# Decode attention with its gradients: Wq's rows kept beside the zeros of the fills, all moments in one tile, V of one group read again

## The chip, the cores and the metric

The kernel runs on one core of a Trainium2 chip. The metric is the device time of one execution in microseconds. Below, PE is TensorE (the matmuls), DVE VectorE, ACT ScalarE, POOL GpSimd and SP SyncE. DMA transfers are issued from the queues of SP, ACT and POOL, and 16 DMA engines carry them all. SBUF has 128 partitions.

## The reference

A transformer block for one token (D = 448) and its gradients. The forward pass, cut to what matters:

```python
W = min(4096, max(256, Sk // 4))               # window of 4096 out of Sk = 32768
q = x_norm @ wq                                # 16 heads of 256, 8 groups of K and V
k, v = k_cache[:, :, Sk - W:], v_cache[:, :, Sk - W:]
p = softmax(q k^T / 16);  o = p v
h  = x + o @ wo
h2 = h + ((norm(h) @ w_gate) * (norm(h) @ w_up)) @ w_down
```

The outputs are h2 and the gradients of x, of both caches and of the five weights. The gradients of the caches (out_2 for K, out_3 for V) have the caches' full size, 8 groups of 32768 x 256 in bf16, 134 MB each. They differ from zero only in the last 4096 positions of each group; the other 28672 have to be written as zeros. That is 235 MB of the 281 MB that the kernel writes.

## The kernel before

**Fills.** The tile `zeros` is [128, 8192] in bf16, 16 KB a partition (line 75). DVE sets its partitions 32 to 95 to zero (L77). A fill (L81) is one DMA that writes a stretch of zeros: its source are the 16 partitions 32, 36, ..., 92 (`ALL`, line 85), each repeated, and one DMA packet is one row of 16 KB. Fifteen of the sixteen regions (a group of out_2 or out_3, 14.7 MB each) are one DMA each on SP's queue. The sixteenth is dealt out in unequal parts per DMA engine, some on SP and some on POOL (`deal`, `deal_all`, `deal_rest`, lines 93 to 117); `deal_rest(0)` is issued after out_0 and `deal_rest(1)` after the last other store.

**SBUF.** One large tile, BIG, is cut into slots of 16 KB a partition. Slots 0 to 7 hold V of groups 0 to 7, slots 8 and 9 alternate for K (`KS = 8`); slot 4 on holds Wq at the start, when V of the later groups isn't there yet. Behind the slots lie a ring of small buffers and 896 columns of Wq that stay (`wq_kept`, KW).

**Stage 1** (0 to about 250 us). Wq is loaded in two DMAs on SP ahead of the fills and one on ACT (lines 67 to 69). In the layout of Wq each partition has 28 KB, seven rows of 2048 columns (NI = 7, HQ = 2048). Layernorm, then q in 112 matmuls (L306). For every group g: scores (K transposed by PE, L341, then L346), softmax, and `moments(g)`, which sums V^T (p K) over the window in 32 steps into a 256 x 512 product (L398), together with o and the mean of K (L401, L404). The loads of K and V go through POOL's queue, in program order, each when its slot is free. The products of the groups 4 to 7 are kept in `Mt` [128, 4, 2, 512]; those of groups 0 to 3 are spread in quarters over the partitions 0 to 31 and 96 to 127 of `zeros`, which no fill reads (`quarter`, L414 and L415).

**Stage 2** (to about 420 us). Wo, the two gate weights and w_down are loaded into the slots of K (`load_wo`, `load_wd`); out_0; then the gradients back to dh, dO and dq. `to_rows` and the broadcasts (L557, L570, L627) bring columns into rows. The quarters are copied back into `Mq` (L585). dq uses the moments (L612).

**Stage 3** (to about 667 us). For each group, 32 matmuls make the rows of dK and dV (`d_ps`, L764) into a pair of slots (`PAIR`), which two DMAs on POOL store. Beside them, `during` deals the outer products that are the gradients of the weights over the steps of the loop, one instruction after each matmul, and their stores go to POOL's queue. The gradient of x needs Wq once more: two loads on POOL in steps 2 and 3 (`dxn_load`), eight products on DVE (L658) in steps 3 and 4.

**Order.** The order on each engine is that of the program, except where `issue_after` names a predecessor. `io_load` chains the loads of POOL.

Of the kernel before, what the change touches and what calls it, by code (L numbers as in the profile page):

```python
# [14 lines left out]
D = 448  # L15
NI = 7
# [14 lines left out]
NZ = (Sk - W) * Dh // (128 * ZW)  # L31


KS = 8
TAIL = 10 * SLOT
KW = 896
RING = TAIL + 6016
SIZE = RING + KW
# [4 lines left out]
def kernel(  # L43
# [21 lines left out]
    wq_sb = BIG[:, 4 * SLOT:4 * SLOT + NI * HQ]  # L65
    wq_kept = BIG[:, RING:SIZE]
    for c0, c1 in ((KW, 4 * HQ), (4 * HQ, NI * HQ)):
        FILL.dma_start(out=wq_sb[:, c0:c1], in_=flat_rows(A_wq)[:, c0:c1])
    S_.dma_start(out=wq_kept, in_=flat_rows(A_wq)[:, 0:KW])

    def wq_at(i, c0, n):
        c = i * HQ + c0
        return wq_kept[:, c:c + n] if c < KW else wq_sb[:, c:c + n]

    zeros = const.tile([128, ZW], bf16)
    for p in (32, 64):
        V_.memset(zeros[p:p + 32, :], 0.0)  # L77
# [7 lines left out]
    ALL = slice(32, 93, 4)  # L85
    for g in range(G):
        for o in (out_2, out_3):
            if (g, o) != (G - 1, out_3):
                fill(FILL, region(o, g), ALL, 8 * NZ, ZW)
# [30 lines left out]
    GQ = G // 2  # L120
    Mt = const.tile([128, GQ, 2, 2 * Dh], bf16)
    ME = 4 * Dh

    def quarter(a):
        p = 96 * (a // 2)
        return zeros[p:p + 32, :].rearrange("p (g b c) -> p g b c", b=2, c=ME)[:, :, a % 2, :]
# [11 lines left out]
    Vw = [slot_kv(g) for g in range(G)]  # L138
# [27 lines left out]

    load_K(0)
# [11 lines left out]
    ones_f = const.tile([128, 128], f32)  # L179
    V_.memset(ones_f[:], 1.0)  # L180
# [23 lines left out]
    Par = const.tile([2, 2, 128], bf16)  # L204
    nc.gpsimd.memset(Par[:], 0.0)
    for i2 in range(2):
        pv = Par[:, i2, :].rearrange("s (m e) -> s m e", e=2)
        nc.gpsimd.affine_select(out=pv, in_=pv, compare_op=ALU.not_equal, fill=1.0, base=-i2,
                                pattern=[[0, 64], [1, 2]], channel_multiplier=2 * i2 - 1)
# [14 lines left out]
    def rows_to_half(row):  # L224
        t = ps.tile([128, NI], f32, tag="tmp", bufs=1)
        xe = small.tile([1, 2, 128], f32, tag="R", name="xe")
        for i in range(NI):
            c = xe[:, i % 2, :]
            V_.tensor_copy(out=c.rearrange("o (m r) -> o m r", r=2), in_=half_cols(row, i))
            P_.matmul(t[:, i:i + 1], lhsT=c, rhs=ones_f[0:1, 0:1], start=True, stop=True)  # L230
        return t
# [12 lines left out]
    def total(parts, n):  # L244
        t = ps.tile([128, n], f32, tag="tmp", bufs=1)
        P_.matmul(t[:], lhsT=ones_f[:], rhs=parts, start=True, stop=True)
        return t
# [24 lines left out]
    def layernorm_bwd(Pp, xh, rstd, extra, gain, tag):  # L272

        st = small.tile([128, 2], f32, tag="lb_st", bufs=1)
        V_.reduce_sum(out=st[:, 0:1], in_=Pp, axis=AX)
        jk = small.tile([128, NI], f32, tag="lb_j", bufs=1)
# [3 lines left out]
        t = small.tile([128, NI], f32, tag="lb_t", bufs=1)  # L280
# [21 lines left out]

    q_ps = ps.tile([128, 2, 16], f32, tag="tmp", bufs=1)
    for b in range(16):
        for i in range(NI):
            P_.matmul(q_ps[:, :, b], lhsT=wq_at(i, b * 128, 128), rhs=xx1[:, i, :], start=(i == 0), stop=(i == NI - 1))  # L306
# [52 lines left out]
    def softmax(g):  # L359
# [10 lines left out]
        P_.matmul(nb[:], lhsT=ones_f[0:2, :], rhs=gd[:], start=True, stop=True)  # L370
# [13 lines left out]
    def moments(g):  # L384
# [26 lines left out]
        if g < GQ:  # L411
            for a in range(4):
                q = quarter(a)[:, g, :].rearrange("p (f c) -> p f c", f=2)
                S_.copy(out=q[:, 0, :], in_=MT[0][32 * a:32 * a + 32, :])  # L414
                V_.tensor_copy(out=q[:, 1, :], in_=MT[1][32 * a:32 * a + 32, :])  # L415
        else:
            S_.copy(out=Mt[:, g - GQ, 0, :], in_=MT[0][:])
            V_.tensor_copy(out=Mt[:, g - GQ, 1, :], in_=MT[1][:])
# [34 lines left out]
    for g in range(G):  # L453
# [3 lines left out]
        if g + 3 < G:  # L457
            load_V(g + 3)
        if g == G - 2:
            load_wo(0, 18)  # L460
        if g == 0:
# [4 lines left out]
            P_.matmul(t[:], lhsT=ones_f[0:1, :], rhs=go_f, start=True, stop=True)  # L466
            S_.copy(out=dh2_bc[:], in_=t[:])
    load_wo(18, 32)
# [85 lines left out]
    def to_rows(blocks, src, nb, b0, n):  # L554
        t = ps.tile([2, 4, 128], f32, tag="tmp", bufs=1, name="t")
        for j in range(n):
            P_.matmul(t[:, j, :], lhsT=src[:, b0 + j:b0 + j + nb + 1:nb], rhs=ident_bf[:], start=True, stop=True)  # L557
        evac(blocks, t[:, 0:n, :])

    P2 = const.tile([128, 2, NI], f32)  # L560
    for w, w_sb in ((0, wg_sb), (1, wu_sb)):
        r = small.tile([2, HF], bf16, tag="R", name="r")
        r_m = r[:].rearrange("s (j m) -> s m j", m=NI)
        for b0 in (0, 4):
            n = min(4, NI - b0)
            to_rows(r_m[:, b0:b0 + n, :], dgu[:, w, :], NI, b0, n)
        for i2 in range(2):
            for x in range(0, HF, D):
                bc = ps.tile([128, D], f32, tag="tmp", bufs=1, name="bc")
                P_.matmul(bc[:], lhsT=Par[:, i2, :], rhs=r[:, x:x + D], start=True, stop=True)  # L570
                evac(bc2[w][:, i2, x:x + D], bc[:])
# [11 lines left out]
    Mq = wu_sb[:, 0:GQ * ME].rearrange("p (g c) -> p g c", c=ME)  # L583
    for a in range(4):
        S_.copy(out=Mq[32 * a:32 * a + 32], in_=quarter(a))  # L585
# [4 lines left out]
    doT_f = const.tile([128, 32], f32)  # L590
# [9 lines left out]
    q_rows = zeros[0:H, 0:Dh]  # L600
    do_rows = zeros[0:H, Dh:2 * Dh]
    rows16(qT, q_rows, SCALE)
    rows16(doT, do_rows, 1.0)

    dq_ps = ps.tile([128, 32], f32, tag="tmp", bufs=1, name="dq_ps")
    for h in range(H):
        for dk in range(2):
            for hf in range(2):
                c0 = (h % 2) * Dh + dk * 128
                g = h // 2  # L610
                m = Mq[:, g, hf * 2 * Dh + c0:hf * 2 * Dh + c0 + 128] if g < GQ else Mt[:, g - GQ, hf, c0:c0 + 128]
                P_.matmul(dq_ps[:, 2 * h + dk:2 * h + dk + 1], lhsT=m, rhs=doT[:, 2 * h + hf:2 * h + hf + 1],  # L612
                          start=(hf == 0), stop=(hf == 1))
# [6 lines left out]
    late = Mt[:].rearrange("p g f c -> p (g f c)")  # L620
    dq_bc = late[:, 0:2 * HQ].rearrange("p (i c) -> p i c", i=2)
    for b1 in range(0, 16, 4):
        r = small.tile([2, 4, 128], bf16, tag="R", name="r")
        to_rows(r[:], dq[:], 16, b1, 4)
        for i2 in range(2):
            bc = ps.tile([128, 512], f32, tag="tmp", bufs=1, name="bc")
            P_.matmul(bc[:], lhsT=Par[:, i2, :], rhs=r[:].rearrange("s b c -> s (b c)"), start=True, stop=True)  # L627
            evac(dq_bc[:, i2, b1 * 128:b1 * 128 + 512], bc[:])
    tps_cm.__exit__(None, None, None)
# [17 lines left out]
    Pq = const.tile([128, NI + 1], f32)  # L647
    wq2 = [slot(3 + i // 4)[:, (i % 4) * HQ:(i % 4 + 1) * HQ] for i in range(NI)]

    def wq_from(i):  # L650
        return 0 if i else KW

    def dxn_load(i0, i1):
        c = wq_from(i0)
        IO.dma_start(out=slot(3 + i0 // 4)[:, c:(i1 - i0) * HQ], in_=flat_rows(A_wq)[:, i0 * HQ + c:i1 * HQ])

    def wq_product(w, i, c, n):
# [164 lines left out]
```

## Time and profile before

| | |
|---|---|
| median of 3 runs | 778.72 us (778.43 to 779.66) |
| the profiled execution | 779.32 us, its span 777.5 us |
| busy: PE, DVE, ACT, POOL | 468.0, 402.0, 177.1, 43.3 us |
| TensorE's granted clock, mean | 0.657 |
| DMA | 330.44 MB, mean 425 GB/s |
| queue of SP | 230.94 MB |
| queue of POOL | 98.59 MB |
| HBM read, written | 49.15 MB, 280.59 MB |

In the profile a group of instructions is named by its line (L764), engine, operation and tile. The table of 40 slices gives the busy share of each engine in tenths, the clock that TensorE was granted, and the busy share and rate of the DMA engines. The queues' rows give packets, MB and the time that the packets took as a share of the 16 engines' span. A row of a DMA issue ends with the microseconds from issue to landing.

### The profile page before, as it was taken

To read this page: it belongs to the slowest core of one execution; us is meant where nothing else is said; L and a number is where in the kernel's file an instruction comes from. 1 tells how busy PE (TensorE), PEld (TensorE's weight loads), DVE (VectorE), ACT (ScalarE), POOL (GpSimd) and SP (SyncE) were. 2 spreads that over 40 slices of the span, in tenths; PEclk is the share of its full clock that TensorE was granted. 3 is DMA by queue.
4 is the path that set the end of the run, shared out by engine and by line. 5 is a ranking of instruction groups with operands and counts; after the bars stand their busy time and mean duration, and the time that the engine had idled before them with its cause. 6 is when DMAs were issued, how large, how long until landed. Compare 5 with 4: busy or idle time off the path is not lost.

```text
span 777.5 us, 10855 instructions
## 1 busy us (share of the span) xinstructions
PE 468.0 (60%) x4375; PEld 257.5 (33%) x4420; DVE 402.0 (52%) x1179; ACT 177.1 (23%) x278; POOL 43.3 (6%) x88
## 2 busy tenths in 40 slices
PE   4798898899899612234076998980957598200000
PEld 3654554565555311113052443430333232000000
DVE  5477677677667311255954656667577377200000
ACT  0322322321120000034333444440413244100000
POOL 3000000000000000010000001000001010100000
PEclk9998998999999855555555555555555555555555
DMA  9999999999999999999999999999999999999998
GB/s 363 427 425 428 426 425 430 428 426 428 424 428 429 429 430 430 433 430 430 424 428 430 430 429 430 428 427 431 428 430 429 429 427 431 430 433 432 428 429 349
DMA packets 25683, 330.44 MB, mean 425 GB/s; under 512 B 3069, under 2 KB 3199, under 8 KB 5046
## 3 DMA queue, kind: packets, MB, share of 16 engines
q1 hardware_dynamic: 14557, 230.94, 69.6%
q0 software_dynamic: 10928, 98.59, 30.1%
q8 instruction: 34, 0.56, 0.3%
q10 hardware_dynamic: 148, 0.23, 0.1%
q14 instruction: 16, 0.12, 0.0%
HBM read 49.15 MB, written 280.59 MB: 424 GB/s over the span
## 4 chain that ended last, share of the span: by engine, by line
PE 40%; DMA 28%; DVE 13%; issue 4%; ACT 2%; another core or an unknown queue 2%; POOL 0%; POOLq 0%; DVEq 0%; ACTq 0%
PE MT L398 12%; DMA out_dram<-BIG 10%; PE tr L341 8%; PE d_ps L764 7%; DMA BIG<-in_B_w_down_dram 7%; DMA BIG<-in_A_wq_dram 6%; DMA BIG<-in_A_k_cache_dram 4%; DVE BIG L588 2%; PE sT L346 2%; DMA BIG<-in_A_wo_dram 2%; DVE BIG L574 1%; PE dp L346 1%; DVE zeros L415 1%; ACT BIG L291 1%
## 5 line engine op out<-in xcount | busy, mean ns | idle before, releaser
L764 PE MATMUL d_ps<-BIG 32*128 32x512 bf16 x256 | 121.8, 607 | 41.3 <-ACT BIG L291 23.9
L398 PE MATMUL MT<-BIG 128*128 128x512 bf16 x467 | 140.4, 409 | 2.1 <-DVE BIG L394 0.4
L394 DVE TENSOR_SCALAR BIG<-BIG,pf 128x256 bf16<-128x256 bf16 x512 | 114.3, 282 | 29.0 <-PE MT L398 26.0
L291 ACT CAST BIG<-d_ps 128x512 bf16<-128x512 f32 x156 | 88.9, 587 | 154.9 <-PE d_ps L764 121.6
L341 PE MATMUL tr<-ident_bf,BIG 128*128 128x128 bf16 x1024 | 113.1, 268 | 14.7 <-DVE doW L588 12.6
L341 PEld LDWEIGHTS <-BIG 128*128 128x128 bf16 x1024 | 80.8, 120 | 43.4 <-issue 41.4
L293 DVE COPY BIG<-tr 128x1024 bf16<-128x1024 bf16 x92 | 63.3, 688 | 43.6 <-PE tr L341 43.3
L293 DVE CAST BIG<-d_ps 128x512 bf16<-128x512 f32 x100 | 68.0, 684 | 16.5 <-DMA out_dram<-BIG 8.2
L291 ACT COPY BIG<-tr 128x1024 bf16<-128x1024 bf16 x36 | 36.4, 1012 | 127.8 <-PE tr L341 120.5
L346 PEld LDWEIGHTS <-BIG 128*128 128x128 bf16 x1024 | 37.4, 102 | 80.1 <-DVE BIG L293 53.3
L401 PEld LDWEIGHTS <-BIG 128*128 128x128 bf16 x512 | 42.2, 99 | 52.9 <-issue 16.9
L401 PE MATMUL acc<-pT_all,BIG 128*128 128x2 bf16 x512 | 45.0, 164 | 16.6 <-DVE kbar L420 15.0
L398 PEld LDWEIGHTS <-BIG 128*128 128x128 bf16 x512 | 40.5, 103 | 23.8 <-issue 16.8
L404 PE MATMUL acc<-pT_all,BIG 128*128 128x2 bf16 x512 | 44.3, 164 | 0.0
L764 PEld LDWEIGHTS <-BIG 32*128 32x128 bf16 x256 | 21.3, 113 | 65.9 <-issue 46.4
L346 PE MATMUL dp<-doT,BIG 128*128 128x2 bf16 x512 | 24.4, 168 | 12.2 <-DVE BIG L293 11.4
L521 DVE CUSTOM_DVE_ANT_0 dh_bc<-BIG,dh_bc 128x448 bf16<-128x448 bf16 x14 | 8.7, 624 | 44.1 <-DMA BIG<-in_B_w_down_dram 43.8
L404 PEld LDWEIGHTS <-BIG 128*128 128x128 bf16 x512 | 30.1, 96 | 0.9
L542 PE MATMUL y<-BIG,hh_bf 128*1 128x448 bf16 x14 | 5.9, 565 | 29.7 <-DMA BIG<-in_B_w_down_dram 29.0
L346 PE MATMUL sT<-qT,BIG 128*128 128x2 bf16 x512 | 22.3, 165 | 0.8 <-ACT BIG L291 0.6
L658 DVE CUSTOM_DVE_ANT_0 BIG<-BIG,Mt 128x2048 bf16<-128x2048 bf16 (+2 forms) x8 | 16.1, 2017 | 8.0 <-DMA BIG<-in_A_wq_dram 7.1
L745 DVE TENSOR_TENSOR BIG<-r_ps,mrow 96x1024 bf16<-96x1024 bf16 (+2 forms) x15 | 18.3, 1221 | 1.4 <-PE r_ps L750 1.1
(186 smaller groups left out, 369.1 us busy)
## 6 DMA issues: line engine op xcount, KB each, us to landing
out_dram<-zeros SPq DMA_DIRECT2D x15, 14336.0 KB, 146.7
out_dram<-BIG POOLq DMA_DIRECT2D x16, 2048.0 KB, 42.7
BIG<-in_A_v_cache_dram POOLq DMA_DIRECT2D x8, 2048.0 KB, 23.5
BIG<-in_A_k_cache_dram POOLq DMA_DIRECT2D x12, 1024.0 KB, 14.7
out_dram<-zeros SPq DMA_DIRECT2D x1, 6144.0 KB
out_dram<-BIG POOLq DMA_DIRECT2D x6, 896.0 KB, 39.0
BIG<-in_A_k_cache_dram POOLq DMA_DIRECT2D x2, 2048.0 KB, 25.4
out_dram<-zeros POOLq DMA_DIRECT2D x2, 1680.0 KB, 77.9
```

What stands on the lines that cost most here:

```text
L291: S_.copy(out=out, in_=in_)
L293: V_.tensor_copy(out=out, in_=in_)
L341: P_.transpose(tr[:, i, dh, :], x_at(g, 4 * q + i)[:, dh * 128:(dh + 1) * 128], ident_bf[:])
L346: P_.matmul(out_ps[:, 4 * q + i, :], lhsT=xt[:, i, dh, :], rhs=vecT[:, 4 * g + dh:4 * g + dh + 3:2], start=(dh == 0), stop=(dh == 1))
L394: V_.tensor_scalar(out=pk[:, i, h, :], in0=K[:, t, :], scalar1=pf[:, t, h:h + 1], scalar2=None, op0=ALU.mult)
L398: P_.matmul(MT[hf][:], lhsT=v_at(g, t)[:, hf * 128:(hf + 1) * 128], rhs=pk[:, i, :, :].rearrange("p h d -> p (h d)"), start=(t == 0), stop ...
L401: P_.matmul(acc[:, 2 * hf:2 * hf + 2], lhsT=v_at(g, t)[:, hf * 128:(hf + 1) * 128], rhs=pT_all[:, g, t, :], start=(t == 0 and hf == 0), st ...
L404: mm = P_.matmul(acc[:, 4 + dk:7 + dk:2], lhsT=K[:, t, dk * 128:(dk + 1) * 128], rhs=pT_all[:, g, t, :], start=False, stop=(t == T - 1), s ...
L588: V_.tensor_tensor_reduce(out=wg_sb[:, 0:D], in0=parked.get(b, wo_b(b)), in1=dh_bc[:], scale=1.0, scalar=0.0, op0=ALU.mult, op1=ALU.add, a ...
L658: V_.tensor_tensor_reduce(out=w, in0=w, in1=dq_bc[:, i % 2, c:HQ] if c else dq_bc[:, i % 2, 0:w.shape[-1]], scale=1.0, scalar=0.0, op0=ALU ...
L745: V_.tensor_tensor(out=rows[p0:p1], in0=r_ps[p0:p1, :].unsqueeze(1).to_broadcast([p1 - p0, 8, 128]), in1=mrow[p0:p1, :].unsqueeze(2).to_br ...
L764: mm = P_.matmul(d_ps[:].rearrange("p w d -> p (w d)"), lhsT=rows[32 * k:32 * k + 32, a, :], rhs=R[32 * k:32 * k + 32, :], start=True, sto ...
```

## The change

`zeros` gets 28 KB a partition (NW = 7 x 2048 columns). The 112 partitions that no fill reads hold their rows of Wq for the whole run. The rows of the 16 partitions that the fills read are loaded into `odd`, the second half of the tile of the moments, on the partitions 32 to 95 in four small DMAs; once at the start and, since the moments of groups 4 to 7 overwrite them, once more after dq. q therefore has two more matmuls per block, with a vector that picks these rows, and dx adds their part by a selection. The Wq loads of stage 3 go, and the nine products with Wq move to step 6.

`Mt` holds the moments of all groups, so the quarters and the copy back go. BIG has one slot less (`KS = 7`): V of group 7 is loaded in halves into the slot of K of group 6 during and after the moments of group 6, and read again into slot 3 in stage 3. Wo is loaded in 9 and 23 blocks. Five of the fills (numbers 5 to 9) use rows of 28 KB; the others keep 16 KB. The gradients of the weights are made in larger tiles. Some small tiles are shared, and dgu is brought into rows in quarters.

```diff
-TAIL = 10 * SLOT
-KW = 896
+KS = 7
+TAIL = 9 * SLOT
 RING = TAIL + 6016
...
-    wq_sb = BIG[:, 4 * SLOT:4 * SLOT + NI * HQ]
-    wq_kept = BIG[:, RING:SIZE]
-    for c0, c1 in ((KW, 4 * HQ), (4 * HQ, NI * HQ)):
-        FILL.dma_start(out=wq_sb[:, c0:c1], in_=flat_rows(A_wq)[:, c0:c1])
-    S_.dma_start(out=wq_kept, in_=flat_rows(A_wq)[:, 0:KW])
...
+    zeros = const.tile([128, NW], bf16)
+    FILL.dma_start(out=zeros[0:32, :], in_=wq_rows[0:32, :])
+    S_.dma_start(out=zeros[96:128, :], in_=wq_rows[96:128, :])
+    Mt = const.tile([128, G, 2, 2 * Dh], bf16)
+    late = Mt[:].rearrange("p g f c -> p (g f c)")
+    odd = late[:, 2 * HQ:4 * HQ]
+    wq_odd = A_wq.rearrange("a b -> (a b)")[32 * NW:96 * NW].rearrange("(e h k c) -> e h k c", h=NI, k=4, c=HQ)
+    def load_odd(eng):
+        for k in range(4):
+            eng.dma_start(out=odd[32 + k:96:4, :].rearrange("p (h c) -> p h c", h=2), in_=wq_odd[:, 0:2, k, :])
+    load_odd(FILL)
     for p in (32, 64):
-        V_.memset(zeros[p:p + 32, :], 0.0)
+        V_.memset(zeros[p:p + 32, 0:ZW], 0.0)
+    V_.memset(zeros[32:64, ZW:NW], 0.0)
+    S_.activation(out=zeros[64:96, ZW:NW], in_=one[64:96, 0:1].to_broadcast([32, NW - ZW]), func=ACT.Copy, scale=0.0)
+    for p in (0, 96):
+        V_.memset(odd[p:p + 32, :], 0.0)
+    for k in (1, 2, 3):
+        S_.dma_start(out=zeros[32 + k:96:4, :], in_=wq_rows[32 + k:96:4, :])
...
+    LONG = range(5, 10)
     for g in range(G):
...
+                f = NW if 2 * g + k in LONG else ZW
+                fill(FILL, region(o, g), ALL, FL // f, f)
...
+    def load_V_half(g, h):
+        t = slice(h * T // 2, (h + 1) * T // 2)
+        io_load(Vw[g][:, t, :], A_v_cache[0, g, Sk - W:, :].rearrange("(p t) d -> p t d", t=T)[:, t, :])
...
+            P_.matmul(q_ps[:, :, b], lhsT=odd[:, h * HQ + b * 128:h * HQ + (b + 1) * 128], rhs=xo[:, h, :], start=False, stop=(h == 1))
...
-        if g < GQ:
-            for a in range(4):
-                q = quarter(a)[:, g, :].rearrange("p (f c) -> p f c", f=2)
-                S_.copy(out=q[:, 0, :], in_=MT[0][32 * a:32 * a + 32, :])
-                V_.tensor_copy(out=q[:, 1, :], in_=MT[1][32 * a:32 * a + 32, :])
...
+            if c == 8 and g == G - 2:
+                load_V_half(G - 1, 0)
+            if c == 8 and g == G - 1:
+                load_wo(0, 9)
+        S_.copy(out=Mt[:, g, 0, :], in_=MT[0][:])
+        V_.tensor_copy(out=Mt[:, g, 1, :], in_=MT[1][:])
...
         if g == G - 2:
-            load_wo(0, 18)
+            load_V_half(G - 1, 1)
...
-    load_wo(18, 32)
+    load_wo(9, 32)
...
+        for h in range(4):
+            r = small.tile([2, HF // 4], bf16, tag="R", name="r")
+            t = ps.tile([2, NI, 32], f32, tag="tmp", bufs=1, name="t")
+            to_rows(r[:].rearrange("s (j m) -> s m j", m=NI), t[:], [dgu[:, w, m::NI] for m in range(NI)], 32 * h)
+            for i2 in range(2):
+                bc = ps.tile([128, HF // 4], f32, tag="tmp", bufs=1, name="bc")
+                P_.matmul(bc[:], lhsT=Par[:, i2:i2 + 128], rhs=r[:], start=True, stop=True)
+                evac(bc2[w][:, i2, h * HF // 4:(h + 1) * HF // 4], bc[:])
...
-    for a in range(4):
-        S_.copy(out=Mq[32 * a:32 * a + 32], in_=quarter(a))
...
+    load_odd(IO)
...
     during = {
...
+        2: [o67_job(slot(2), 0, 0, 7)],
+        3: [o5_job(slot(2), 0)],
+        4: [o5_job(slot(4), 16)],
+        5: [o4_job(slot(2), 0, 4), o4_job(slot(4), 4, 7)],
+        6: [o8_job(half(2, 0), 0), o8_job(half(2, 1), 7), dxn()],
+        7: [dx_out()],
     }
-    loads = {2: (0, 4), 3: (4, 7)}
-    begin = {3: 8}
+    begin = {3: 4, 5: 8, 6: 8}
...
-                if t == 26 and s in loads:
-                    dxn_load(*loads[s])
+                if t == 26 and s == 3:
+                    Vw[G - 1] = slot_kv(3)
+                    IO.dma_start(out=Vw[G - 1], in_=A_v_cache[0, G - 1, Sk - W:, :].rearrange("(p t) d -> p t d", t=T))
```

## The prediction

> **What bounds the kernel now.** I read the page's table of 40 slices first, then its DMA queues, then busy time by stage, then the POOL queue's timeline, and last the transfers that open the run.
>
> The header and the slices:
>
> ```profile
> span 777.5 us, 10855 instructions
> ...
> PE   4798898899899612234076998980957598200000
> ...
> DMA  9999999999999999999999999999999999999998
> GB/s 363 427 425 428 426 425 430 428 426 428 424 428 429 429 430 430 433 430 430 424 428 430 430 429 430 428 427 431 428 430 429 429 427 431 430 433 432 428 429 349
> ```
>
> No engine is busy throughout, but the DMA engines are: full in every slice, at 424 to 433 GB/s except in the first (363) and the last (349). The sixteen DMA engines are the bound, and the time is the price of the transfers. The queues give that price:
>
> ```profile
> q1 hardware_dynamic: 14557, 230.94, 69.6%
> q0 software_dynamic: 10928, 98.59, 30.1%
> ...
> q10 hardware_dynamic: 148, 0.23, 0.1%
> ...
> HBM read 49.15 MB, written 280.59 MB: 424 GB/s over the span
> ```
>
> q1 is SP's queue (the fills), q0 POOL's, q10 ACT's. 69.6% of 777.5 us for 230.94 MB is 2.34 us per MB; 30.1% for 98.59 MB is 2.37. I use 2.35.
>
> How far compute is from the bound, by stage (columns: stretch, its length, busy PE, weight loads, DVE, ACT, POOL, TensorE's clock, DMA share, GB/s):
>
> ```profile
> 0.00:20.00 20.00, 8.47 (x42) 8.24 (x43) 11.59 (x29) 1.54 (x2) 6.00 (x20) 1.00 0.92 365
> 660.00:680.00 20.00, 5.01 (x13) 1.17 (x11) 4.84 (x7) 3.78 (x7) 2.31 (x4) 0.50 1.01 433
> 680.00:700.00 20.00, 0.00 (x0) 0.00 (x0) 0.00 (x0) 0.00 (x0) 1.20 (x2) 0.50 1.00 428
> 740.00:760.00 20.00, 0.00 (x0) 0.00 (x0) 0.00 (x0) 0.00 (x0) 0.00 (x0) 0.50 1.01 429
> 760.00:780.00 20.00, 0.00 (x0) 0.00 (x0) 0.00 (x0) 0.00 (x0) 0.00 (x0) 0.51 0.70 298
> ```
>
> POOL's timeline has its last pair of stores issued here:
>
> ```profile
> 666.50 1.05 POOL L788 DMA_DIRECT2D out_dram<-BIG  x2 [14.16 <-issue]
> ```
>
> From 666.5 us to the end, 111 us, the DMA engines work off queues and nothing computes. At 0.428 MB/us that is 47 MB, of which POOL's queue holds some 9 (two 2 MB stores, 2.5 MB of late fills, what was queued before); SP's holds the rest. So compute could end about 80 us later before SP's queue ran dry under it.
>
> The start, whose sources are the issue rows and the SP timeline:
>
> ```profile
> BIG<-in_A_wq_dram SPq DMA_DIRECT2D x1, 1824.0 KB, 8.9
> BIG<-in_A_wq_dram ACTq DMA_DIRECT2D x1, 224.0 KB, 15.2
> 0.76 0.86 SPq L68 DMA_DIRECT2D BIG<-in_A_wq_dram  x2
> 5.16 729.40 SPq L83 DMA_DIRECT2D out_dram<-zeros  x18
> ```
>
> The trace's packet records add: first packet at 3.0 us (SP), first of POOL's at 7.1, first fill at 19.4; a 16 KB packet takes 611 ns, an 8 KB one 309, a 4 KB one 159, and a packet starts 4 ns before its predecessor on the engine ends.
>
> **The change, part by part, in DMA time.** *Bytes.* Removed: the opening Wq loads (1824 + 1536 + 224 KB) and the two of the second phase (1824 + 1536 KB), 6944 KB. Added: 112 rows of 28 KB (3136 KB), the rows of the fill's own partitions twice (4 transfers of 16 rows by 8 KB, 512 KB each time), V of group 7 once more (2048 KB): 6208 KB. Net -736 KB or 0.75 MB: **-1.8 us**. All these have 16 or a multiple of 16 rows, so I spread them evenly over the engines.
>
> *Packets.* Joining two 8 KB packets into one of 16 saves 2 x 309 - 611 = 7 ns, or 3 after the overlap. The five fills with 28 KB rows have 32 packets per engine and not 56: 5 x 24 x (3 to 7) = 0.4 to 0.8 us. The outputs in larger tiles, Wq in fewer rows and V in halves come to about 40 fewer per engine, 0.1 to 0.3. Should a 28 KB row be cut into two packets, the first saving is only 8 packets a fill, and 0.1 remains. I take **-0.6 us**.
>
> *The 32-row loads at the start.* Rows 0-31 go out on SP and 96-127 on ACT, 917 KB each, two 28 KB packets per engine apiece. By 611 ns for 16 KB a packet is 1.06 us and all is in the byte term. But every load of before has 128 rows, so each DMA engine had partitions of its own; here two engines write into each group of four. No row shows that. Bounds: nothing more, or each of the four packets at double length, +4.2 us. The nearest row is the opening of the Wq load: its first ten packets took 1172 ns on average, against 545 for an undisturbed one of 14 KB, so a packet at the start can take twice its price. I charge that in full for SP's two, which run from 3.0 us when POOL's queue is not there yet (+2.1), and half for ACT's two, which run among POOL's (+1.1): **+3.2 us**. By the Trainium skill ("SBUF — State Buffer", section "Door 1: The DMA port swizzle (why `[64,N]` ≈ `[32,N]`)") partitions 0 to 31 reach 8 of SBUF's 16 DMA ports, 189 GB/s at 1 MiB against 328 for 128 partitions; by that the two loads would cost about 4.2 us extra (estimate) and the sum would be +2.0. No run here shows it yet.
>
> *The rest of the start.* SP then issues four small loads and waits for the memsets: two of 3.47 us with 0.9 before each, so the first fill can go at about 10 us, not 19. POOL's queue begins at 7.1 with 10 MB issued by 4.1 and covers that; if POOL alone could not fill the engines it would cost up to 1 us. ACT zeroes 32 x 6144, then issues three loads that wait for DVE's memsets up to about 13 us; behind them in ACT's queue stand the layernorm's square root and the evacuations, and POOL's queue is not involved. **0**, cover: POOL's loads.
>
> *Compute.* q gets 32 more matmuls (166 ns each, 5 us) and waits for ACT's loads: it was ready at 25.8 us, now some us later. V of group 7 goes into K's slot in halves and Wo in 9 + 23 blocks, not 18 + 14: 9 x 112 KB more behind the last moments, +5 us. The long fills run at about 260 to 470 us; a POOL packet that alternates with them waits 1.06, not 0.61. Four to eight packets per engine in each of five loads in series (the chain has 24.4, 8.5, 9.2, 9.1 us for w_down alone): +15 to +25. The regroup of dgu in quarters has 12 steps and not 6 per weight, about 1 us each: +10. The nine products with Wq (2.0 us each, DVE) move from steps 3 and 4 to step 6: DVE +18 there, but the chain's 47.8 us for the second Wq load is gone, of which the pair stores hid perhaps half; the quarter copies go too. Sum: compute ends 0 to 40 us later. Cover: the 80 us above, so **0**.
>
> *End.* The fills dealt out per engine at the end are unchanged. Packets of instruction code (34 of 16 KB at 0.93 us) may become one more: **+0.2**.
>
> Sum: -1.8 - 0.6 + 3.2 + 0.2 = +1.0. Against the profiled execution, 779.32 (its span and 1.8 around it), that is 780.3; that execution lies 0.6 above the median of 778.72, so for the median **779.7 us**.
>
> **Rivals.** *A: the 32-row loads cost nothing extra.* For it: DMA share 1.01 in all stretches, whatever mix of loads and stores was in flight. Against: none of these had two engines on one partition group. -1.8 - 0.6 + 0.2 = -2.2: 776.5.
>
> *B (slower): each 28 KB packet of these loads takes twice its time,* because two engines share each group of partitions and stay in step, on both queues. Place: 3 to 12 us. -1.8 - 0.6 + 4.2 + 0.2 = +2.0, and up to 0.7 more for idle engines between SP's small loads before POOL's arrive, of which I take 0.4: 781.1. It decides from an extra of 3.8 on. For it: the doubled first packets; against: q10 and q1 could take turns on the two sets of partitions.
>
> *C (slower): compute ends too late.* The ACT loads of the fill partitions' neighbours get stuck behind a fill. For it: ACT's small Wq load, 8 packets of 74 ns per engine, landed 15.2 us after issue and began at 7.0 although issued at 1.6, while SP's transfers were being dealt out. Behind a whole fill it could be 50 us; q, scores and all that follows shift by that, and with 0 to 40 above the 80 us are reached. Past that point each us of lateness is a us of time: 0 to 15 us, centre 785. Against: it needs both delays near their upper ends.
>
> **How the numbers follow.** A run of this kernel can be told from no change at about 0.2%, 1.56 us. Forecast (net within +-1.56; own range 778.0 to 780.3): 0.38. A: 0.26, all but its upper edge faster. B: 0.22 and C: 0.14, slower. So faster 0.26, same 0.38, slower 0.36. The range cuts off the lower tail of A (776.3) and the upper part of C (784).
>
> **What would show it.** The page's HBM read falls to 48.4 MB and q10 rises to about 2.3 MB. Right: the first slice at about 290 GB/s (3.2 us x 428 over its 19.4 us less than 363), the middle at 425 to 433, DMA full to the end. Under A the first slice stays near 363. Under B it is at about 255. Under C the last POOL store is issued after about 745 us and DMA digits below 9 appear near the end. I would be wrong if the middle slices change their GB/s, or if one DMA engine ends far behind the others.

## The result, and the profile after

The changed kernel takes 784.58 us (median of 4 runs, 784.14 to 784.98), the kernel before 778.71 on the same chip: a ratio of 1.0073, 95% interval 1.0056 to 1.0090. It is slower by 5.9 us, where I had forecast 1.0 us and a range that ended at 784.0. The profiled execution took 784.74 us with a span of 782.9, against 779.32 with 777.5; the spans differ by 5.35 us.

The header, slices and queues of the changed kernel's page:

```profile
span 782.9 us, 11090 instructions
...
DMA  9999999999999999999999999999999999999996
GB/s 285 425 427 425 427 429 426 427 428 424 432 424 425 438 426 434 432 433 434 427 426 437 426 423 420 431 430 433 429 425 429 429 433 428 428 431 429 430 431 270
...
q1 hardware_dynamic: 12589, 228.94, 68.6%
q0 software_dynamic: 10400, 97.77, 29.8%
q10 hardware_dynamic: 148, 2.30, 0.9%
...
HBM read 48.40 MB, written 280.59 MB: 420 GB/s over the span
```

The middle is as before, full and at 420 to 438 GB/s, and the bytes fell as counted (HBM read 49.15 to 48.40 MB). Only the two ends differ: the first slice has 285 GB/s and not 363, the last 270 and not 349.

POOL's timeline (start, length, line, and in brackets the idle time before and what ended it): in the kernel before, the store of out_0 and the first pair of stores of stage 3,

```profile
332.57 0.51 POOL L546 DMA_DIRECT2D out_dram<-dh_bc  x1 [13.71 <-ACT dh_bc L545]
...
445.99 1.05 POOL L788 DMA_DIRECT2D out_dram<-BIG  x2 [48.32 <-issue]
```

and in the changed kernel the same two and the last instructions:

```profile
372.26 0.51 POOL L566 DMA_DIRECT2D out_dram<-dh_bc  x1 [16.15 <-ACT dh_bc L565]
...
521.21 1.05 POOL L802 DMA_DIRECT2D out_dram<-BIG  x2 [61.65 <-DVE BIG L301]
...
739.76 1.08 POOL L802 DMA_DIRECT2D out_dram<-BIG  x2 [5.35 <-issue]
740.83 2.46 POOL L95 DMA_DIRECT2D out_dram<-zeros  x4
```

The first pair goes 75 us later than before, the last one 73 us later (666.50 before). The loop of stage 3 itself kept its length (219 against 221 us), so the delay arose ahead of it.

Where the 5.35 us are, by the packet and instruction records of the two traces (a packet's record doesn't name its engine; an engine's last packet follows from stringing the packets together by their ends and starts):

| | before | after | difference, us |
|---|---|---|---|
| MB moved by 30 us | 11.37 | 9.80 | 1.57 MB at 0.4275 MB/us, the rate of the full slices: +3.7 |
| MB in all | 330.44 | 329.70 | 0.74 MB at 2.35 us per MB: -1.7 |
| end of an engine's last packet, mean of 16 | 774.15 | 776.09 | +1.94, the two lines above |
| end of the very last packet | 776.21 | 778.34 | +2.13, so +0.19 of spread |
| from there to the end of the span | 1.34 | 4.56 | +3.22 |

The last line is the surprise. At the end of the program POOL executes a DRAIN, and every engine waits for it. The views leave this instruction out; its times here are from the instruction records of the traces. In the kernel before, the last data packet of POOL's queue ended at 764.9 us, POOL's drain returned at 774.0, and SP's fills ended at 776.2: the drain was hidden. In the changed kernel the last packets of the two queues end together (POOL 778.34, SP 777.99). SP's waits for its transfers are over at 779.7, POOL's drain returns only at 782.1, 3.8 us after its queue's last data packet, and nothing is left to cover it. SP's list of waits shows this as a longer wait for the other engines on the last line of the program (us in total, times, the longest; the list names PE's queue, but by the instruction records the wait ends with POOL's drain). Before:

```profile
SPq L817 <- PEq L817: 0.6, 2, 0.5
```

The change:

```profile
SPq L831 <- PEq L831: 3.0, 2, 2.5
```

### The profile page after: what moved, and what is told of

The parts are those of the page before. It is cut to its first block, busy times and chain, and to the rows that moved or that the text cites. A ratio compares the mean times of both kernels' runs of the same rounds, so it can differ in the third digit from the quotient of the medians.

```text
span 782.9 us, 11090 instructions
## 1 busy us (share of the span) xinstructions
PE 471.6 (60%) x4506; PEld 260.9 (33%) x4506; DVE 403.7 (52%) x1190; ACT 162.0 (21%) x270; POOL 42.3 (5%) x86
## 2 busy tenths in 40 slices
DMA packets 23188, 329.70 MB, mean 421 GB/s; under 512 B 3149, under 2 KB 3151, under 8 KB 4486
## 3 DMA queue, kind: packets, MB, share of 16 engines
HBM read 48.40 MB, written 280.59 MB: 420 GB/s over the span
## 4 chain that ended last, share of the span: by engine, by line
PE 36%; DMA 31%; DVE 14%; issue 7%; ACT 4%; another core or an unknown queue 3%; POOL 1%; POOLq 0%; DVEq 0%; ACTq 0%
DMA BIG<-in_A_k_cache_dram 10%; DMA out_dram<-BIG 9%; DMA BIG<-in_B_w_down_dram 8%; PE d_ps L777 8%; PE tr L363 8%; PE MT L420 8%; ACT BIG L299 3%; DMA BIG<-in_A_wo_dram 3%; DVE BIG L602 3%; DVE BIG L663 2%; DMA BIG<-in_A_v_cache_dram 2%; DVE BIG L591 2%; DVE BIG L301 2%; PE dp L368 2%
## 5 line engine op out<-in xcount | busy, mean ns | idle before, releaser
L420 PE MATMUL MT<-BIG 128*128 128x512 bf16 x512 | 142.2, 391 | 4.1 <-DMA BIG<-in_A_v_cache_dram 4.1
L416 DVE TENSOR_SCALAR BIG<-BIG,pf 128x256 bf16<-128x256 bf16 x512 | 111.6, 281 | 34.3 <-PE MT L420 32.1
L301 DVE COPY BIG<-tr 128x1024 bf16<-128x1024 bf16 x92 | 63.3, 688 | 53.2 <-PE tr L363 50.3
L301 DVE CAST BIG<-d_ps 128x512 bf16<-128x512 f32 x100 | 68.0, 684 | 39.4 <-DMA out_dram<-BIG 33.4
L238 PE MATMUL t<-one,xe 1*128 1x1 f32 x42 | 11.2, 332 | 24.5 <-DVE xe L237 24.0
```

What stands on the lines that cost most here:

```text
L301: V_.tensor_copy(out=out, in_=in_)
L416: V_.tensor_scalar(out=pk[:, i, h, :], in0=K[:, t, :], scalar1=pf[:, t, h:h + 1], scalar2=None, op0=ALU.mult)
L420: P_.matmul(MT[hf][:], lhsT=v_at(g, t)[:, hf * 128:(hf + 1) * 128], rhs=pk[:, i, :, :].rearrange("p h d -> p (h d)"), start=(t == 0), stop ...
```

## The experiments

Times are medians beside the kernel before on the same chip. "Pair" is the issue of the last pair of stores, "tail" the time from the last data packet to the end of the span; both are from the profiled execution.

| kernel | time, before | ratio, interval | pair | tail |
|---|---|---|---|---|
| the change | 784.58, 778.71 | 1.0073, 1.0056 to 1.0090 | 739.8 | 4.6 |
| opening loads over 128 partitions | 781.15, 778.56 | 1.0029, 1.0018 to 1.0039 | 744.1 | 4.5 |
| before, Wq in loads of 32 partitions | 788.03, 778.56 | 1.0126, 1.0108 to 1.0145 | | 1.5 |
| before, the last packets on POOL | 781.38, 778.56 | 1.0034, 1.0021 to 1.0046 | | 4.2 |
| late fills of POOL ahead of two pairs | 784.38, 778.56 | 1.0077, 1.0063 to 1.0091 | 747 | 4.1 |
| no 28 KB rows in the fills | 782.21, 778.63 | 1.0042, 1.0030 to 1.0055 | 690.9 | 1.5 |
| second load of Wq's odd rows later | 784.42, 778.63 | 1.0073, 1.0060 to 1.0086 | 727.1 | 4.3 |
| the last two together | 781.31, 778.63 | 1.0033, 1.0021 to 1.0045 | 691.3 | 1.5 |
| 16 KB rows, V not read again | 776.90, 778.74 | 0.9978, 0.9966 to 0.9990 | 676.8 | 1.5 |
| 128 partitions, 16 KB rows, odd rows later | 778.79, 778.74 | 1.0002, 0.9994 to 1.0011 | 705.0 | 2.8 |
| no 28 KB rows, V of group 7 read once | 776.90, 778.74 | 0.9978, 0.9966 to 0.9990 | 676.8 | 1.5 |
| eight-row opening loads | 784.63, 778.63 | 1.0075, 1.0063 to 1.0088 | 693.1 | 1.6 |
| all of Wq in one load, copy of zeros | 784.13, 778.74 | 1.0068, 1.0055 to 1.0081 | 694.7 | 1.4 |
| the same, q early | 785.06, 778.61 | 1.0082, 1.0069 to 1.0096 | 691.9 | 1.4 |
| all of Wq in one load, zeros by a multiplication | 776.73, 778.75 | 0.9972, 0.9962 to 0.9983 | 680.1 | 1.5 |

### The start: the form of the loads

The changed kernel, with the bytes of its two 32-row loads sent into 128 partitions of a free slot. It leaves out these 64 rows of Wq, which POOL sets to zero:

```diff
-    FILL.dma_start(out=zeros[0:32, :], in_=wq_rows[0:32, :])
-    S_.dma_start(out=zeros[96:128, :], in_=wq_rows[96:128, :])
+    q4 = NW // 4
+    flat = A_wq.rearrange("a b -> (a b)")
+    for n, (eng, p) in enumerate(((FILL, 0), (S_, 96))):
+        eng.dma_start(out=BIG[:, 4 * SLOT + n * q4:4 * SLOT + (n + 1) * q4],
+                      in_=flat[p * NW:(p + 32) * NW].rearrange("(p x) -> p x", p=128))
...
+    for p in (0, 96):
+        nc.gpsimd.memset(zeros[p:p + 32, :], 0.0)
```

> The changed kernel, but the two 32-row loads of the opening (917 KB each, SP and ACT) bring the same bytes into 128 partitions of a slot that is free then; the 64 rows of Wq that they held are zeroed by POOL, so q and the gradient of x lack their part of Wq. Theory 1 (two DMA engines write into each group of four partitions, so these loads and POOL's K packets beside them take double): the 28 KB packets of 2.0 to 2.3 us and the K packets of 1.0 to 1.4 us go, the first slice rises from 285 to about 360 GB/s, and the time falls by 3.7 us to 780.9. Rival (the start is slow because it is cut into many small transfers and waits for memsets): 784 to 785, the first slice stays below 300.

Measured: 781.15, 3.4 us less than the change. Its slices:

```profile
GB/s 356 431 427 429 427 426 429 425 427 430 426 425 428 432 431 429 437 428 436 430 432 430 426 427 422 426 432 430 431 428 427 431 428 430 430 429 431 431 432 280
```

The first slice is back at 356 (285 in the change, 363 before), and 11.33 MB are moved by 30 us. The last slice is still low, 280, with a tail of 4.5 us. So the start and the end are two separate losses.

The other way round, the kernel before with its two opening loads of Wq on SP cut by partitions, the same bytes:

```diff
-        FILL.dma_start(out=wq_sb[:, c0:c1], in_=flat_rows(A_wq)[:, c0:c1])
+        for p in range(0, 128, 32):
+            FILL.dma_start(out=wq_sb[p:p + 32, c0:c1], in_=flat_rows(A_wq)[p:p + 32, c0:c1])
```

> The kernel before, but each of its two opening Wq loads on SP is cut into four of 32 partitions; same bytes, same data. Theory 1: 3.4 MB that took 8.1 us of the DMA engines go at half speed wherever nothing else is beside them, +4 to +8 us: 783 to 787, first packets of about 1.1 us and not 0.55. Rival: no more than six further handshakes, below +1: 778.7 to 779.7.

Measured: 788.03, +9.5 us, beyond the 4 to 8 that I expected and far from the rival's 1. Its slices:

```profile
GB/s 248 348 425 430 424 427 428 426 430 424 428 428 426 432 427 430 433 428 428 428 429 431 428 428 432 428 428 429 431 430 429 429 427 433 430 431 430 430 429 357
```

The first two slices have 248 and 348 GB/s where the kernel before has 363 and 427. 7.77 MB are moved by 30 us, not 11.37: 8.4 us. The packets of the first four of these loads (14592 bytes) take 0.92 us in the median instead of 0.545, and POOL's 16 KB packets of the first 20 us 0.90 instead of 0.61. That is what I had not priced: the neighbours pay as well.

### The end: POOL's queue last

The kernel before with nothing changed but who issues the 24 last packets per engine, POOL instead of SP:

```diff
-    deal_all(24, ZW)
     deal_all(8, 1224)
...
             deal(IO, 9, 7, 15)
+            fill(IO, last[used[0]:used[0] + 16 * 24 * ZW], ALL, 24, ZW)
+            used[0] += 16 * 24 * ZW
```

> The kernel before, but the 24 packets per engine that SP deals out of the last region are issued by POOL after everything else; the work of each engine is the same. Theory 2: POOL's queue ends last, the end after the last packet grows from 1.3 to about 4.6 us, +3.2: 781.9. Rival: 778.7, since no engine has more to do.

Measured: 781.38, +2.8 us, 0.5 less than expected. The engines' last packets end on average where they did (773.96 against 774.15), the last of POOL's at 775.37, and the tail is 4.2 us and not 1.3. This shows the price of the drain alone, in a kernel whose bytes and computation are those of the kernel before.

In the changed kernel I first tried to have POOL's queue empty earlier by issuing its late fills before the last two pairs:

```diff
-    with tc.issue_after(tail.ins):
-        deal_rest(1)
...
+        if s == 5:
+            with tc.issue_after(tail.ins):
+                deal_rest(1)
```

> The changed kernel, but the last deals of zeros on POOL are issued after the stores of step 5 and not after those of step 7. Theory 2 (POOL's queue is the last to finish, and POOL's drain at the end of the program returns 3.7 us after its last packet, where SP's wait returns 0.7 after): POOL's last packet falls from 778.3 to about 770, the drain lies beside SP's last fills, and the end after the last packet falls from 4.6 to about 1.4 us: 781.4. Rival (the end is late because the engines have unequal work left): 784 to 785.

Measured: 784.38, a miss. The fills were issued earlier, but POOL's stores then waited for them (the pair went at 747 us, 13.6 us of it waiting for a fill), and POOL was still last: 778.42, SP 768.56. Moving work within POOL's queue doesn't shorten the queue.

### Why compute is 73 us late

Two suspects: the 28 KB rows of five fills, and the second load of the odd rows, four DMAs in POOL's queue that wait for dq.

```diff
-    LONG = range(5, 10)
+    LONG = range(0)
```

> The changed kernel with rows of 16 KB in all fills. Theory (the five fills with 28 KB rows save 0.4 us of DMA time, but each POOL packet beside them waits 1.06 and not 0.61 us, which delays compute by 15 to 25 us): the last pair of stores is issued at 715 to 725 and not at 739.8. If POOL's queue then ends before SP's, its drain is hidden: 784.6 + 0.4 - 3.2 = 781.8; if it still ends last, 785.0. Rival (long rows do not delay anything): the last pair at 740, 785.0.

Measured: 782.21, a gain of 2.4 us. Its POOL timeline:

```profile
348.27 0.51 POOL L566 DMA_DIRECT2D out_dram<-dh_bc  x1 [12.49 <-ACT dh_bc L565]
...
471.89 1.05 POOL L802 DMA_DIRECT2D out_dram<-BIG  x2 [36.27 <-issue]
...
690.93 1.08 POOL L802 DMA_DIRECT2D out_dram<-BIG  x2 [6.36 <-issue]
692.00 2.46 POOL L95 DMA_DIRECT2D out_dram<-zeros  x4
```

The store of out_0 goes 24 us earlier than in the change, the pairs 49. POOL's last data packet ends at 756.1 us, SP's at 778.17, and the tail is 1.5 us and not 4.6. The engines' mean end is the same (776.14 against 776.09), so what is gained is the drain, now hidden.

Where the 49 us were, from the lists of waits of PE and DVE (engine, line, what it waited for: us in total, times, the longest). The change:

```profile
PE y L562 <- DMA BIG<-in_B_w_down_dram: 37.2, 3, 13.1
...
DVE dh_bc L541 <- DMA BIG<-in_B_w_down_dram: 57.3, 4, 20.0
DVE BIG L301 <- DMA out_dram<-BIG: 33.4, 3, 25.2
```

Without the long rows:

```profile
PE y L562 <- DMA BIG<-in_B_w_down_dram: 27.6, 3, 9.9
...
DVE dh_bc L541 <- DMA BIG<-in_B_w_down_dram: 36.5, 4, 10.0
...
DVE BIG L301 <- DMA out_dram<-BIG: 9.5, 2, 7.1
```

Beside the long rows PE and DVE wait 10 and 21 us more for the chained loads of w_down; both wait for the same loads, so the two don't add up, and 24 us is what has come together by the store of out_0. That the prediction had. The third line it did not have: L301, which fills a pair's slot, waits 24 us more for an earlier store from that slot, on its way through the same queue. One wait of 25.2 us just ahead of the first pair is nearly all of it, and 24 and 25 are the 49.

The Trainium skill ("DMA: Bandwidth & Descriptors", section "Queues, rings and completion order") says that a DMA engine takes turns between queues packet by packet. The traces agree: with both queues full and rows of 16 KB (502 to 520 us without the long rows), the engines took 229 packets of POOL's and 241 of SP's, each 0.61 us; a row of 28 KB takes 1.06 us, and a packet of POOL's that waits for one waits that much longer for its turn.

The second suspect, the odd rows behind the first stores of the gradient of w_up:

```diff
-    load_odd(IO)
...
         for _ in job:
             pass
+    load_odd(IO)
```

> The changed kernel, but the second load of the fill partitions' Wq rows is issued on POOL after the first two stores of the gradient of w_up and not before them. Theory (these stores stand behind the load, which waits for dq, and step 0 of stage 3 waits 27 us for the slots that they free): the wait at 483 to 510 us shrinks to 10 us or less, the last pair of stores moves from 739.8 to 715 to 725, and the time falls by up to 3.2 us if POOL's queue no longer ends last: 781.4 to 784.5. Rival (the wait has another cause): the last pair at 740, 784.6.

Measured: 784.42. The pair goes 12.7 us earlier, at 727, which isn't enough: POOL's last data packet is at 777.55, the tail 4.3 us. Both edits together:

> Both: 16 KB rows in all fills and the second load after the stores. Theory: compute ends 35 to 50 us earlier, the last pair of stores is issued at 690 to 705, POOL's queue ends before SP's, and the end after the last packet falls from 4.6 to 1.4 us: 784.6 + 0.4 - 3.2 = 781.8. Rival (the late end comes from the engines' unequal work): 785.0.

Measured: 781.31, pair at 691.3, as without the long rows alone: the odd rows' load held nothing up once the stores ran freely. Between 691 and 727 us lies the point from which the drain shows; a kernel further down, with its last pair at 705, shows part of it.

### The price of the bytes, and what is left

The kernel without the long rows, and without the second load of V of group 7:

```diff
-                    IO.dma_start(out=Vw[G - 1], in_=A_v_cache[0, G - 1, Sk - W:, :].rearrange("(p t) d -> p t d", t=T))
```

> The changed kernel with 16 KB rows in all fills and without the second read of V of group 7 (the slot keeps V of group 3, so the gradients that need V of group 7 are not those of the reference). Theory (the time is the price of the bytes, 2.35 us per MB): 2.1 MB less, 782.2 - 4.9 = 777.3. Rival (compute or a queue bounds the end): less than half of that.

It leaves out the V that the gradients of group 7 need. Measured: 776.90, 5.3 us less for 2.1 MB, where 2.35 us per MB give 4.9. The single runs of the two kernels scatter by more than this difference (2.4 and 3.2 us), so a byte is worth its DMA time here, within what can be told.

The wide opening loads, the 16 KB rows and the later odd rows in one kernel, which takes both losses away at once:

> Both corrections to what the change lost: the two 32-row loads' bytes go to 128 partitions (their 64 rows of Wq are zeroed by POOL, so q and the gradient of x lack that part), all fills have 16 KB rows, and the second load stands after the stores. What the change would be worth without the slow opening and without the late end: 781.3 - 3.7 to 4.2 = 777.1 to 777.6. If it is well above, a third loss is left unexplained.

Measured: 778.79, 1.2 us above the expectation. The engines end at 772.50 on average, 1.65 us before the kernel before, which is the bytes. But the two memsets on POOL that stand in for the 64 rows made q late (52.6 us), the pair went at 705 and POOL's last data packet was at 770.09; its drain returned at 776.0 where SP's last packet was at 773.97, so 1.3 us of it still show. POOL's queue was 3.9 us ahead of SP's, and that was not enough to hide the drain.

### Versions with the computation whole

Three ways to get rid of the 32-row loads lost the time again in another place. First, the same 64 rows as eight loads of 8 rows each (every fourth partition) on POOL's queue, with K of group 0 on SP:

```diff
-    FILL.dma_start(out=zeros[0:32, :], in_=wq_rows[0:32, :])
-    S_.dma_start(out=zeros[96:128, :], in_=wq_rows[96:128, :])
...
+    for j in range(4):
+        for p in (0, 96):
+            io_load(zeros[p + j:p + 32:4, :], wq_rows[p + j:p + 32:4, :])
```

> As before this one (16 KB rows, second load after the stores), and the opening without loads of 32 adjacent rows: K of group 0 goes first on SP, and the 64 rows of Wq come as eight loads of 8 rows, four partitions apart, on POOL. Data and output are the whole reference. Theory: no two engines write into one group of four partitions, the 3.7 us of the start come back: 781.8 - 3.7 = 778.1, about the kernel before or slightly under it. Rival (many small loads are slow as such): 781 or more.

Measured: 784.63, a miss. The eight loads of 8 rows did not spread evenly over 16 engines: these end at 775.16 on average, the last at 780.64, 5.5 us behind, and most packets of 28 KB took 1.06 to 1.7 us. Eight engines end at 773 or before and eight at 778 or after, as if all eight loads had gone to the same half of the engines (8 packets of 1.06 us are 8.5 us); that is not shown.

Second, all 128 rows of Wq in one load, q straight from them, then 16 rows of zeros copied over the fill partitions from a blank slot, and only then the fills:

```diff
-    FILL.dma_start(out=zeros[0:32, :], in_=wq_rows[0:32, :])
-    S_.dma_start(out=zeros[96:128, :], in_=wq_rows[96:128, :])
+    FILL.dma_start(out=zeros[:], in_=wq_rows)
...
-    load_odd(FILL)
...
+    FILL.dma_start(out=zeros[32:96:4, :], in_=blank[32:96:4, :])
```

> 16 KB rows and the second load after the stores, and a third opening: all 128 rows of Wq come in one load of 128 partitions, q is computed from them, and only then are the 16 rows of the fills overwritten with zeros by a DMA from a zeroed slot; the fills start behind that, at about 28 us. The whole reference is computed. Bytes against the changed kernel: +0.46 MB of Wq, +0.46 of zeros, -0.52 of the first small loads, net +0.4 MB or +0.9 us. Theory (only a load over 128 partitions gives every DMA engine its own): 781.3 - 3.7 to 4.2 + 0.9 = 778.0 to 778.5, no small packet above 0.7 us at the start. Rival (POOL's loads alone cannot keep the engines full until 28 us): a dip below 420 GB/s in the second slice and 780 or more.

Measured: 784.13. Three in four of its packets of 28 KB take 1.06 to 1.08 us (the first of each engine up to 2.2) and POOL's beside them 0.61: neither the size of a row nor the queue is what doubles them, it is the block of 32 adjacent partitions. Nor is it few partitions as such: ACT's three small loads in the changed kernel write 16 rows each, every fourth partition from 33 to 95, and their packets take 1.06 us too. But the first fill starts at 42 us, POOL's loads run dry at 35, and the engines are empty for 4.9 us between, taken together. The third kernel makes q early:

```diff
-    for p in (32, 64):
-        V_.memset(blank[p:p + 32, :], 0.0)
+    V_.memset(blank[32:64, :], 0.0)
...
-    gX = const.tile([128, NI], f32)
-    V_.tensor_copy(out=gX[:], in_=rows_to_half(go_bf)[:])
     rstd1, xh1, xf1, xx1 = layernorm(xX[:], "ln1")
...
-    FILL.dma_start(out=zeros[32:96:4, :], in_=blank[32:96:4, :])
+    FILL.dma_start(out=zeros[32:96:4, :], in_=blank[32:64:2, :])
```

> The kernel with all 128 rows of Wq in one load, but q made early: the blank rows are one memset on 32 partitions (one of the two 6.0 us memsets goes), their 16 rows are copied from partitions 32, 34, ..., 62, and the gradient's row is brought into columns behind the fills and no longer ahead of the layernorm (6.3 us). q should be ready at about 24 us instead of 37.4, the zero copy should end at about 27 and the fills should start at about 28, before POOL's loads run dry at 35. If the seven empty microseconds were all that kept the time of that kernel up (theory): 784.1 - 6.3 = 777.8, just below the kernel before (778.7), engines full from 5 to 770 us, tail of about 1.5 us. Rival (the gap was not the cause, something else in that layout costs the time): 782 to 784.

Measured: 785.06, no gain, although q was ready at 24 us as expected. SP's list of waits says why (L298 is the copy of zeros):

```profile
SPq L298 <- DMA BIG<-in_A_k_cache_dram: 26.5, 1, 26.5
SPq L298 <- DMA BIG<-in_A_v_cache_dram: 9.5, 2, 4.8
```

The copy reads BIG, into which K and V are being loaded, and was issued only behind the last of them, at 37.3 us, though they lie in other slots. The engines were empty for 4.8 us again. So the copy was the wait, and the last kernel has none: it multiplies the tile by 0 on the 16 fill partitions and by 1 on the others.

```diff
-    V_.memset(blank[32:64, :], 0.0)
...
-    FILL.dma_start(out=zeros[32:96:4, :], in_=blank[32:64:2, :])
+    keep = const.tile([128, 1], f32)
+    V_.reduce_sum(out=keep[:], in_=ident_f[:, 32:96:4], axis=AX)
+    V_.tensor_scalar(out=keep[:], in0=keep[:], scalar1=-1.0, scalar2=1.0, op0=ALU.mult, op1=ALU.add)
+    V_.tensor_scalar(out=zeros[:, 0:3 * HQ], in0=zeros[:, 0:3 * HQ], scalar1=keep[:, 0:1], scalar2=None, op0=ALU.mult)
+    S_.activation(out=zeros[:, 3 * HQ:NW], in_=zeros[:, 3 * HQ:NW], func=ACT.Copy, scale=keep[:, 0:1])
```

> The kernel with all 128 rows of Wq in one load and q made early, but without the blank rows and their copy: after q, DVE (6144 columns) and ACT (8192 columns) multiply the tile by 0 on the 16 fill partitions and by 1 on the others, each about 6 to 7 us. No memset ahead of the layernorm, so q should be ready at about 20 us and the first fill should start at about 28, before POOL's loads run dry at 35. Bytes: the kernel with the copy moved 329.97 MB, less 0.46 for the copy = 329.51, 0.81 MB less than the kernel before. Theory (the opening's price was the form of the loads, and an empty DMA in the runs that avoided it): 30 us moves some 11.4 to 11.8 MB, no idle stretch, and 778.7 - 1.9 (bytes) + 0.2 (tail of 1.5 us against 1.3) = 777.0. Rival (holding Wq in the fills' tile costs the time in whatever form): 781 to 784.

Measured: 776.73 us against 778.75, a ratio of 0.9972 (0.9962 to 0.9983): faster than the kernel before, and 7.9 us faster than the change. Its page:

```profile
span 775.0 us, 10990 instructions
...
DMA  9999999999999999999999999999999999999998
GB/s 380 409 427 426 429 426 427 425 429 424 429 427 430 429 430 430 429 432 428 428 430 430 426 429 429 430 428 431 430 427 432 430 430 430 430 430 431 429 432 353
...
HBM read 48.33 MB, written 280.59 MB: 424 GB/s over the span
```

Its two multiplications on the timelines:

```profile
22.19 1.82 DVE L299 TENSOR_SCALAR zeros<-zeros,keep 128x6144 bf16<-128x6144 bf16 x1 [2.73 <-PE q_ps L293]
...
22.30 7.12 ACT L300 ACTIVATE zeros<-zeros,keep 128x8192 bf16<-128x8192 bf16 x1 [3.43 <-PE q_ps L293]
```

They end at 24.0 and 29.4 us, before POOL's loads run dry, so no DMA engine is idle; 11.76 MB are moved by 30 us (11.37 before), the last pair goes at 680, and the tail is 1.5 us. The bytes give -1.9 of the measured -2.0 us. So holding Wq in the fills' tile is worth its saved bytes, if the start is loaded over 128 partitions and POOL's drain returns before SP's fills end. This kernel also has the 16 KB rows and the later second load of the odd rows.

## Why the prediction was wrong

**The step that failed is "Compute", with "End +0.2".** I took compute as 0 to 40 us later under a cover of 80 us, at a price of 0. It came 73 us later, still inside the cover as I had defined it: the DMA engines never ran out of work. But I had the wrong edge. What shows first is not SP's queue running dry but POOL's drain returning last: it came 3.4 to 4.1 us after the last data packet where the two queues ended together or POOL's ended last, while SP's waits were over 0.5 to 0.7 us after its last packet where SP's ended last. In these kernels the drain is hidden at 25 us of lateness (pair at 691, 666.5 before), shows in part at 38 (705) and in full at 61 (727), and in full it costs about 3 us: +3.22 here, +2.8 in the kernel before with only the order of the last packets changed, -2.4 when the long rows go. My sum had no term for the end of the program beyond 0.2.

**The lateness was mis-sized, too.** The long rows made 49 us, not 15 to 25: the chained loads behaved as described (24 us), but I counted loads only, and left out that a pair's slot waits for its earlier store in the same queue (25 us more at L301). Without the long rows 24 us remain at the last pair. The store of out_0 is 15.7 us late there and the first pair 25.9. The first part fits q: it was ready at 40.9 us and not 25.8, after three more memsets of DVE (DVE turns to x at 17.4 us and not at 9.8) and slower steps that bring x and the gradient into columns ahead of q (0.89 us and not 0.45 each), where I had said "some us". What I did name for q, 32 more matmuls at 166 ns, was too dear: the 144 took 4.2 us and the 112 before 3.1, since they overlap. The other 10 us arise between out_0 and the first pair, where I had charged 10 for the regroup of dgu; no run takes that apart.

**32-row loads: right, a little low.** +3.2 taken, 3.7 measured; the first slice was forecast at 290 GB/s and has 285. SP's packets took 2.06 and 2.25 us on average (first and second row of each engine) and ACT's 1.96, against 1.06 undisturbed, so each one about doubles, on both queues, which is rival B's mechanism; and POOL's packets beside them took 0.8 to 1.4 us instead of 0.61, which no rival had. The six profiled executions that keep these loads have 251 to 285 GB/s in their first slice, so this price varies by about 1.5 us. By the rule that I had weighed (the Trainium skill, "SBUF — State Buffer", section "Door 1: The DMA port swizzle (why `[64,N]` ≈ `[32,N]`)"), partitions 0 to 31 reach half of the ports, which gave an estimate of 4.2. The traces agree with it, and the run with Wq in loads of 32 partitions (8.4 us) shows it again on loads that nothing else changed. The packet times that I gave for the start (3.0, 7.1 and 19.4 us) are some 1.3 us later than the records have them from the span's start (1.8, 5.8 and 18.1); no term hangs on that.

**Bytes: right.** HBM read 48.40 MB and q10 2.30 MB as forecast, -1.7 us; the run with both losses removed ended its engines 1.65 us earlier.

**Packets: too high.** -0.6 taken. The engines' mean end moved by 0.05 us with the five long fills in one pair of kernels, and by 0.4 in another (772.08 and 772.50 in the two kernels with wide loads). That is 0 to 0.4, no more than the start varies, and the same rows cost 2.4 us at the end.

**Rivals.** A is out. C named the number (785) and the place, compute too late, but its cause didn't occur: ACT's loads were not stuck behind a fill, the last of their packets started at 21.8 us and the first fill at 23.0. Nor did its price per microsecond: with the last pair at 727, 740 and 747 us the tail is 4.3, 4.6 and 4.1 us, so lateness past the edge costs about 3 us once and not a us each. That C's number fits is luck. The signs I listed for C, a last store after 745 and DMA digits below 9 at the end, came close (739.8, a digit of 6), and the 6 is the drain.

The remainder is small: of the 5.35 us in the two profiled executions all are in the table above; the medians differ by 5.9, since the profiled execution of before lies 0.6 above its median and that of the change 0.2. Two things stay open: the 10 us of lateness between out_0 and the first pair, and why POOL's drain takes so long. Nor does the drain simply move with the last pair: without the long rows it returned at 766.0 us with the last pair at 691, in the kernel before at 774.0 with the pair at 666.5. There POOL's four late fills were issued one by one up to 693 us, each waiting for an earlier store; in the changed kernel all four follow the last pair at once.

## What to carry to other kernels

In a kernel bound by its DMA, ask which queue ends last, and not only when the queues run dry: engine work that is "covered" can bring POOL's drain to the end of the program long before it starves anything. POOL's data should end well before SP's: here 3.9 us were too few, and 11.3 us or more hid the drain in all nine kernels that had them. Load tiles over all 128 partitions, at the start above all: blocks of 32 adjacent rows took about twice their time here and slowed down whatever ran beside them. Longer rows in a bulk queue saved next to nothing (0 to 0.4 us) and delayed the short chain of loads in the other queue by 24 us.

## What the runs showed of the hardware that was not expected

- POOL's drain at the end of the program returns 3.4 to 4.1 us after the last data packet of its queue where that queue ends last or with SP's (3.77, 3.76, 3.35, 4.09 and 3.41 us in five runs). Where SP's fills go on, it takes longer: 5.9 us in one run and 8.2 to 10.2 in nine. In all 15 traces it returns 3.3 to 3.7 us after the last record of POOL's queue, one of 4 bytes, and beside SP's fills these records come up to 6.6 us behind the data. SP's waits for its own last packet are over 0.5 to 0.7 us after it where SP's queue is clearly the last.
- Loads of 32 partitions lengthen the packets of other queues on the same engines: 16 KB from 0.61 us to 0.8 to 1.4 in the changed kernel, and to 0.90 in the median with Wq in loads of 32 partitions.
- Eight loads of 8 rows each did not even out over 16 engines: a spread of 5.5 us between the mean and the last end.
- DVE multiplies 6144 bf16 columns by a value per partition in 1.82 us (3400 columns a us); ACT takes 7.12 us for 8192 (1150 a us). I had given both 6 to 7 us.
